# Casts of half batches 5 to 7 in another order and place, three row squares moved: a windowed attention with an MLP behind it

## The chip, the cores and the metric

The kernel runs on one core of one Trainium2 chip. Its engines are PE (matmul), DVE (VectorE), ACT (ScalarE), POOL (GpSimd) and SP (SyncE); POOL and SP also issue DMAs, each in the order of its own instructions. The metric is the device time of one launch in microseconds, the median of several runs. The kernel before took 351.6 us (three runs: 351.6, 352.7, 348.52).

## What is computed

Inputs are q, k and v of 8 batches, 8 heads, 576 rows and head size 64 in float32, eight global row numbers, and the weights of an MLP (512 to 2048 to 512). Cut to what matters, the reference is:

```
scores = q @ k.T / 8
mask   = (|i - j| <= 32) or i is global or j is global
attn   = softmax(where(mask, scores, -1e9))
x      = attn @ v, the heads of a row side by side     # 4608 x 512
h      = x @ w_in                                      # 4608 x 2048
out    = (h * cos(h)) @ w_out                          # 4608 x 512, float32
```

## The kernel before

A *half* is four of a batch's eight heads; half s is half of batch s // 2, so there are 16. A *pair* is two heads; half s holds pairs 2s and 2s + 1, 32 in all. The MLP works on nine tiles of 512 rows. A *first-layer unit* (`one`) is four matmuls of 128x512 for one of the 16 slices of h of a tile (L764), the cosine on ACT (L770) and the product g on DVE (L771). A *second-layer unit* (`two`) is four matmuls of 128x512 into an output block (L802); each fourth ends the block, which DVE or ACT evicts and SP writes out.

Pairs 0 to 9 take a path of their own and run mostly at the front. For halves 5 to 15 the work of a half is, in order:

- **casts** (`cast_half(s, which)`): for each letter of `which` one DMA on POOL, which reads v, k or q of the half in float32 and writes it in fp16 to device memory. v is L268, k and q are L272.
- **bring** (`bring(s)`), all on SP: a transposing DMA of k into kT (L284) and of q into qT (L285), which wait for k's and q's casts, and then the loads of v's windows for the two pairs (`load_v`, L350 to L357) and of its global rows (`load_vg`, L416), which wait for v's cast. kT and qT have two buffers each.
- per pair `local_k` (L609) and `local_q` (L621): DVE copies the windows out of kT and qT into kw and qb; POOL puts the global rows in their place (L581, L588).
- `scores` (L701 on PE, exponential on ACT at L704 and L709, mask multiply on DVE at L705 and L710, result pm), `values` (L721 on PE, normalised by DVE into xn at L732), `turn_x` (PE transposes xn at L746, DVE evicts it into xT at L748 and L749; behind each fourth pair POOL adds eight copies of global columns into xT, L754).
- `x_squares(s)` (L820): ACT squares the half's xn in place and adds the squares up, for a check at the end. xn has four buffers, one for each half.

The order of all this is written out by hand, as strings of steps that a loop at L1007 reads; each engine gets its instructions in this order and runs them in order, and semaphores join the engines. Step s = 4 reads MID (L50), 5 reads FIFTH (L52), 6 reads SIXTH (L54) and 7 to 15 read ORDER (L48). In them `1` is a first-layer unit and `2` a second-layer unit; `s`, `p`, `x`, `k`, `q` with a letter are scores, values, turn_x, local_k and local_q of pair 2s (`a`), 2s + 1 (`z`), 2s + 2 (`c`) or 2s + 3 (`d`); `n` is `x_squares(s - 1)` and `n1` is `x_squares(1)`; `G` (`casts(s)`) places the global rows of half s + 1 and, from step 6, a gate and the casts of half s + 2 in the order v, k, q; `Z0` to `Z5` build the masks of the second path on DVE; `A0` to `A2` gather the second half of the global rows on POOL; `K6` casts half 6; `B5` brings half 5, and `bring(s + 2)` is also called at the end of each step from 4 on (L1035).

`V10` and `U10` are gates. `hold(10)` (L391) and `hold_x(10)` (L395) are a copy of one element on POOL that waits until local_q, or the values, of pair 10 are done; POOL then goes on to the casts behind it. K5 stands at the end of FRONT, behind the 2 MB load of w_out; K6 stands in MID behind V10; K7 stands in FIFTH behind U10.

The `K` step is an entry of the table at L995, with the order of its three casts:

```
"K": lambda s: cast_half(s, "vkq")
```

Of the kernel before, what the change touches and what calls it, by code (L numbers as in the profile page):

```python
# [17 lines left out]
B, H, S, D = 8, 8, 576, 64  # L18
# [5 lines left out]
G = 8  # L24
# [17 lines left out]
C = G + QB  # L42
# [4 lines left out]

ORDER = "2 kz qz sa 2 2 2 sz pa 1 2 1 2 xa n pz 1 1 G 2 xz 1 1 2 kc qc 1 1"  # L48

MID = ("+ 1 1 1 1 Z0 1 1 1 Z1 1 1 Z2 1 1 A0 n1 1 Z3 1 1 1 Z4 1 1 A1 n2 1 1 1 Z5 A2 1 1 1 n3 B5 1 2 2 g10 g11 kc qc V10 K6 2 2 1 1 2 2 kd qd - 2 2")  # L50

FIFTH = "sa G 2 2 2 2 sz pa 1 1 2 xa U10 K7 pz 2 2 2 kc qc xz n kd qd"  # L52

SIXTH = "sa 2 2 2 2 sz pa 1 1 2 xa pz G 1 1 2 xz n 1 1 D0 2 kc qc D1 1 D2 2 1"  # L54

# [7 lines left out]
def view(ap, *dims):  # L63

    return bass.AP(ap.tensor, ap.offset, [ap.ap[0], *[list(d) for d in dims]])


def dview(ap, offset, *dims):

    return bass.AP(ap.tensor, ap.offset + offset, [list(d) for d in dims])  # L70
# [134 lines left out]
def kernel(  # L205
# [57 lines left out]
    def cast_half(s, which):  # L263

        base = s * 4 * S * D
        for x in which:
            if x == "v":
                nc.gpsimd.dma_start(v16[s * 4 * S : (s + 1) * 4 * S].rearrange("(n r) d -> n (r d)", r=16),  # L268
                                    dview(v, base, (16 * D, 4 * S // 16), (1, 16 * D)))
            else:  # L270
                src, dst = {"k": (k, k16), "q": (q, q16)}[x]
                nc.gpsimd.dma_start(dst[s].rearrange("t (h d) -> t h d", h=4),  # L272
                                    dview(src, base, (D, S), (S * D, 4), (1, D)))
# [41 lines left out]
    def warm(n, tag="s"):  # L315

        t = ps.tile([P, 4, P], FP32, tag=tag, bufs=2 + (tag == "s"))
        for _ in range(n):
            nc.tensor.matmul(t, ones16, view(ones16, (0, 4), (1, P)), start=True, stop=True)
# [436 lines left out]
    def mlp_in(t, f):  # L756
        if f == 0:
            g_of[t] = work.tile([P, NF, TT], FP16, tag="g", name="g")
        g16 = g_of[t]
        tag = "s" if spare[0] and f % 4 > 1 else "h"  # L760
        ph = ps.tile([P, TT], FP32, tag=tag, bufs={"s": 3, "h": 2}[tag], name="ph")
        ph_of.append((ph, g16[:, f]))
        for j in range(NC):
            nc.tensor.matmul(ph, w_in16[:, j, f * P : (f + 1) * P], xT[:, j, t * TT : (t + 1) * TT],  # L764
                             start=(j == 0), stop=(j == NC - 1))

    def mlp_act():
        ph, g = ph_of.pop(0)
        cos = work.tile([P, TT], FP16, tag="cos", bufs=3)
        nc.scalar.activation(cos, ph, AF.Sin, bias=pio2)  # L770
        nc.vector.tensor_tensor(g, cos, ph, ALU.mult)  # L771
# [99 lines left out]
    def one(act=True):  # L871
        for _ in range(1):

            if ins_q and ins_q[0][0] < ready[0] and ins_q[0][0] < outs_q[0][0] + 2:
                t, f = ins_q.pop(0)
                mlp_in(t, f)
                if act:
                    mlp_act()
                ready[1] = t * NF + f + 1
# [22 lines left out]
    with tc.manual_schedule():  # L902
# [85 lines left out]
        def bring(s):  # L988
# [4 lines left out]

        LOCAL = {"k": local_k, "q": local_q}
        OTHER = LOCAL | {"g": globals_kq, "L": load_qk, "W": load_w_in, "v": load_values, "n": x_squares,  # L995
                 "C": cast_vn, "I": row_numbers, "E": early_rows, "w": lambda n: warm(n, "h" if n == 6 else "s"), "y": value_rows, "M": next_values, "S": spread_vg, "V": hold, "U": hold_x, "H": early_globals, "Z": steady_buffers, "f": fill, "r": load_vn, "A": later_rows, "D": later_globals, "O": load_w_out, "K": lambda s: cast_half(s, "vkq"), "B": bring, "m": lambda _: one(False), "t": lambda _: mlp_act()}
        ready[0] = 1
        for step in FRONT.split():
            if step in "+-":
# [2 lines left out]
            f = (STEPS | OTHER)[step[0]]  # L1002
            f(*[int(x) for x in (step[1:] or "0").split(".")])
        ready[0], front[0] = 2, False
        for s in range(4, B * NP // 2):
            outs_by[0] = 8 * (s - 3)
            for step in {4: MID, 5: FIFTH, 6: SIXTH}.get(s, ORDER).split():  # L1007
                if step == "1":
# [19 lines left out]
                else:  # L1028
                    f, pr = (STEPS | OTHER)[step[0]], 2 * s + "azcd".index(step[1])
# [56 lines left out]
```

## Time and profile before

| | |
|---|---|
| median of three runs | 351.6 us |
| the profiled execution | 348.71 us |
| its span, first to last instruction | 346.9 us |
| mean granted clock of PE in it | 0.982 |
| PE busy | 329.1 us, 95% |
| DVE, ACT, POOL busy | 251.1, 241.6, 106.6 us |
| chain that ended last, share of PE | 80% |

A line of a timeline has the start in us from the span's start, the duration in us, the engine, the line of the kernel, the operation, what it writes and reads (out<-in, with partitions x elements), how many were merged, and in brackets how long the engine sat idle before it and what ended that. A line of the waits has the engine and the line that waited, for what, and us in total, times, and the longest. A line of busy times by stretch has the stretch, its length, the busy time of PE, of its weight loads, of DVE, ACT and POOL (number of instructions in brackets), the granted clock, the DMA share and GB/s. SPq is the queue of DMAs that SP issues.

In the profiled execution step 4 begins near 58.7 us, step 5 near 88.6, step 6 near 102.2, step 7 near 117.6; from there each step takes 16.65 us, until the attention ends near 268 us and only second- and first-layer units are left.

### The profile page before, as it was taken

The page shows a single profiled execution, that of the slowest core. Times are in us where ns is not written, and L with a number is a line of the kernel's source. Part 1 is how long each engine was busy: PE and PEld are TensorE (multiplying, and loading weights), DVE is VectorE, ACT ScalarE, POOL GpSimd, SP SyncE. Part 2 cuts the span into 40 slices and gives each one's busy share as a digit, 9 for nine tenths or more (in the row PEclk, how much of TensorE's full clock was granted, in tenths as well). Part 3 has the DMA queues.
Part 4 walks back from the last instruction along what each step waited for, and adds up shares of the span by engine and source line. Part 5 has one row for each costly group of instructions (what it writes and reads, how often), then busy time and mean ns, then how long its engine had stood idle before and what let it go on. Part 6 is the DMA issues. An engine that isn't in the chain of part 4 may idle for free.

```text
span 346.9 us, 8353 instructions
## 1 busy us (share of the span) xinstructions
PE 329.1 (95%) x3153; PEld 171.6 (49%) x3153; DVE 251.1 (72%) x610; ACT 241.6 (70%) x415; POOL 106.6 (31%) x218
## 2 busy tenths in 40 slices
PE   7986979999989999999999999999999999999993
PEld 3565865444444454545454545454545444444442
DVE  6668697987587688878787878788888466556310
ACT  8787684895566896878787777878787866644300
POOL 7846458333252506050705162324001000000000
PEclk9999698999999999999999999999999999999998
DMA  5999996999999999999999999999960001000112
GB/s 79 187 177 160 154 195 85 210 157 117 177 136 198 149 172 128 177 141 196 141 188 142 190 135 200 157 148 161 166 124 4 30 32 60 30 33 30 60 62 69
DMA packets 166275, 44.74 MB, mean 129 GB/s; under 512 B 153828, under 2 KB 161380, under 8 KB 166052
## 3 DMA queue, kind: packets, MB, share of 16 engines
q1 hardware_dynamic: 106244, 26.86, 52.6%
q0 software_dynamic: 59984, 17.28, 51.2%
q8 instruction: 27, 0.44, 0.6%
q14 instruction: 20, 0.16, 0.2%
HBM read 44.41 MB, written 19.17 MB: 183 GB/s over the span
## 4 chain that ended last, share of the span: by engine, by line
PE 80%; DVE 5%; DMA 4%; issue 3%; SPq 3%; ACT 3%; POOL 0%; POOLq 0%; ACTq 0%; DVEq 0%
PE po L802 34%; PE ph L764 34%; PE pv L721 3%; PE st L701 3%; DMA qn<-in_q_dram 2%; SPq L373 2%; PE tx L746 2%; DMA vn<-vg 2%; PE pv L648 1%; DVE g L771 1%; PE po L784 1%; ACT cos L770 1%; PE tx L680 1%; PE bank L597 1%; DVE pm L637 0%
## 5 line engine op out<-in xcount | busy, mean ns | idle before, releaser
L764 PE MATMUL ph<-xT,w_in 128*128 128x512 f16 x576 | 140.4, 382 | 1.1 <-DVE g L771 1.0
L770 ACT ACTIVATE cos<-ph,pio 128x512 f16<-128x512 f32 x144 | 97.1, 687 | 58.1 <-PE ph L764 54.2
L802 PE MATMUL po<-w_out,g 128*128 128x512 f16 x560 | 136.8, 379 | 0.0
L771 DVE TENSOR_TENSOR g<-cos,ph 128x512 f16<-128x512 f16 x144 | 96.5, 685 | 45.8 <-ACT cos L770 43.6
L764 PEld LDWEIGHTS <-w_in 128*128 128x128 f16 x576 | 54.2, 98 | 63.5 <-issue 3.0
L802 PEld LDWEIGHTS <-g 128*128 128x128 f16 x560 | 53.7, 98 | 63.7
L704 ACT ACTIVATE e<-st 128x512 f16<-128x512 f32 x44 | 23.9, 594 | 10.0 <-PE st L701 9.9
L705 DVE TENSOR_TENSOR pm<-e,mask 128x512 f16<-128x512 f16 x44 | 18.8, 427 | 11.7 <-ACT e L704 10.3
L981 POOL COPY gate<-xn 1x1 f16<-1x1 f16 x8 | 1.4, 180 | 81.9 <-DVE xn L732 81.9
L754 POOL COPY xT<-xg 128x4 f16 x48 | 15.6, 325 | 31.7 <-DVE xT L749 29.0
L272 POOL DMA_DIRECT2D q<-in_q_dram x11 | 24.0, 2180 | 0.0
L820 ACT ACTIVATE xn<-xn 128x1536 f16<-128x1536 f16 (+1 forms) x16 | 22.7, 1416 | 0.0
L732 DVE TENSOR_TENSOR xn<-pv,r_all 128x768 f16<-128x768 f32 x22 | 21.1, 958 | 1.0
L807 ACT COPY o<-po 128x512 f32<-128x512 f32 x17 | 10.0, 586 | 14.7 <-PE po L802 14.7
L809 DVE COPY o<-po 128x512 f32<-128x512 f32 x18 | 12.4, 690 | 9.0 <-PE po L802 8.5
L272 POOL DMA_DIRECT2D k<-in_k_dram x11 | 18.1, 1643 | 0.9 <-issue 0.9
L770 ACT ACT_TABLE_LOAD x12 | 15.4, 1283 | 0.2
L636 ACT ACTIVATE e<-st 128x488 f16<-128x488 f32 x20 | 10.5, 578 | 6.4 <-PE st L633 6.4
L704 ACT ACT_TABLE_LOAD x11 | 14.1, 1283 | 0.2
L609 DVE COPY kw<-kT 128x1320 f16<-128x1320 f16 x22 | 14.2, 646 | 0.0
L701 PEld LDWEIGHTS <-kw 64*128 64x128 f16 x484 | 8.4, 95 | 10.7 <-issue 8.1
L581 POOL COPY kw<-kgT 128x88 f16<-128x88 f16 x22 | 12.6, 706 | 0.2 <-ACT kgT L559 0.2
(184 smaller groups left out, 381.2 us busy)
## 6 DMA issues: line engine op xcount, KB each, us to landing
out_dram<-o SPq DMA_DIRECT2D x35, 256.0 KB
vw<-v SPq DMA_DIRECT2D x32, 165.0 KB
v<-in_v_dram POOLq DMA_DIRECT2D x11, 288.0 KB
k<-in_k_dram POOLq DMA_DIRECT2D x11, 288.0 KB
q<-in_q_dram POOLq DMA_DIRECT2D x11, 288.0 KB
vn<-in_v_dram SPq DMA_DIRECT2D x20, 120.0 KB
w_in<-in_moe_w_in_dram POOLq DMA_DIRECT2D x4, 512.0 KB
w_out<-in_moe_w_out_dram POOLq DMA_DIRECT2D x1, 2048.0 KB
```

Source lines behind the costliest of these rows:

```text
L272: nc.gpsimd.dma_start(dst[s].rearrange("t (h d) -> t h d", h=4), dview(src, base, (D, S), (S * D, 4), (1, D)))
L609: nc.vector.tensor_copy(to, view(kT[pr // 2 % 2][:, pr % 2], (QB, NB), (1, W)))
L701: nc.tensor.matmul(st[j // 8 * 2 + h][:, j % 8 * C : j % 8 * C + C], kp[hp, j], qp[hp, j], start=True, stop=True)
L704: nc.scalar.activation(e[:, 0:512], st[h], AF.Exp, scale=scale)
L705: nc.vector.tensor_tensor(view(pm[:, h], (1, 512)), e[:, 0:512], view(mask, (1, 512)), ALU.mult)
L732: nc.vector.tensor_tensor(view(xn, (384, 2), (D, 6), (1, D)), view(pv, (512, 2), (65, 6), (1, D)), view(rp, (6, 2), (1, 6), (0, D)), ALU.mult)
L754: nc.gpsimd.tensor_copy(xT[:, :, bass.ds(pool_idx[g] + b * S, 1)], xg[:, :, g : g + 1])
L764: nc.tensor.matmul(ph, w_in16[:, j, f * P : (f + 1) * P], xT[:, j, t * TT : (t + 1) * TT], start=(j == 0), stop=(j == NC - 1))
L770: nc.scalar.activation(cos, ph, AF.Sin, bias=pio2)
L771: nc.vector.tensor_tensor(g, cos, ph, ALU.mult)
L802: nc.tensor.matmul(po, g16[:, f, s * P : (s + 1) * P], w_out16[:, f], start=(f == 0), stop=(f == NF - 1))
L820: nc.scalar.activation(view(xn, (BP * P, 2), (1, n)), view(xn, (BP * P, 2), (1, n)), AF.Square, accum_out=x_sq[:, s : s + 1])
```

## The change

Three strings change.

```diff
-MID = ("+ 1 1 1 1 Z0 1 1 1 Z1 1 1 Z2 1 1 A0 n1 1 Z3 1 1 1 Z4 1 1 A1 n2 1 1 1 Z5 A2 1 1 1 n3 B5 1 2 2 g10 g11 kc qc V10 K6 2 2 1 1 2 2 kd qd - 2 2")
+MID = '+ 1 1 1 1 Z0 1 1 1 Z1 1 1 Z2 1 1 A0 1 Z3 1 1 1 n1 Z4 1 1 A1 1 1 1 Z5 A2 1 1 1 B5 1 2 2 g10 g11 kc qc V10 K6 n2 2 2 1 1 2 2 n3 kd qd - 2 2'
-FIFTH = "sa G 2 2 2 2 sz pa 1 1 2 xa U10 K7 pz 2 2 2 kc qc xz n kd qd"
+FIFTH = 'sa G 2 2 2 2 sz pa 1 1 2 xa pz 2 2 2 kc qc xz U11 K7 n kd qd'
-"K": lambda s: cast_half(s, "vkq")
+"K": lambda s: cast_half(s, "kqv")
```

- In MID the squares of half 1 move four first-layer units later, behind Z3; those of half 2 move from ahead of six first-layer units to behind K6, ahead of two second-layer units; those of half 3 move from ahead of B5 to behind four second-layer units, ahead of local_k of pair 11.
- In FIFTH the gate and the casts of half 7 move from behind the turn of pair 10 to behind the turn of pair 11, with its eight copies on POOL, and the gate waits for the values of pair 11 in place of pair 10.
- The casts of halves 5, 6 and 7 go out in the order k, q, v. Those of halves 8 to 15 keep v, k, q.

No instruction is added or taken away.

More of the change, by code (lines that the diff above doesn't have):

```diff
@@ L995 @@
         OTHER = LOCAL | {"g": globals_kq, "L": load_qk, "W": load_w_in, "v": load_values, "n": x_squares,
-                 "C": cast_vn, "I": row_numbers, "E": early_rows, "w": lambda n: warm(n, "h" if n == 6 else "s"), "y": value_rows, "M": next_values, "S": spread_vg, "V": hold, "U": hold_x, "H": early_globals, "Z": steady_buffers, "f": fill, "r": load_vn, "A": later_rows, "D": later_globals, "O": load_w_out, "K": lambda s: cast_half(s, "vkq"), "B": bring, "m": lambda _: one(False), "t": lambda _: mlp_act()}
+                 "C": cast_vn, "I": row_numbers, "E": early_rows, "w": lambda n: warm(n, "h" if n == 6 else "s"), "y": value_rows, "M": next_values, "S": spread_vg, "V": hold, "U": hold_x, "H": early_globals, "Z": steady_buffers, "f": fill, "r": load_vn, "A": later_rows, "D": later_globals, "O": load_w_out, "K": lambda s: cast_half(s, "kqv"), "B": bring, "m": lambda _: one(False), "t": lambda _: mlp_act()}
         ready[0] = 1
```

## Prediction

> **What bounds the kernel now.** I read the page first, then the busy times by stretch of the span, then who PE waited for between 52 and 130 us (the stretch in which the changed steps run), then the timelines of the five engines there. The first two show that PE has next to no free time.
>
> ```profile
> span 346.9 us, 8353 instructions
> PE 329.1 (95%) x3153; PEld 171.6 (49%) x3153; DVE 251.1 (72%) x610; ACT 241.6 (70%) x415; POOL 106.6 (31%) x218
> 96.00:104.00 8.00, 6.87 (x79) 3.65 (x78) 7.09 (x15) 4.90 (x8) 5.10 (x9) 1.00 1.53 146
> 153.00:267.00 114.00, 114.00 (x1138) 57.85 (x1137) 94.80 (x214) 89.58 (x145) 31.20 (x68) 1.00 1.40 152
> ```
>
> From 153 to 267 us PE is busy in all of the 114.00 us at a granted clock of 1.00, so nothing done by another engine there sets the end. Between 96 and 104 us 1.13 us of PE are missing. All that PE waited for other engines between 52 and 130 us is this:
>
> ```profile
> PE st L701 <- DVE qb L621: 1.1, 1, 1.1
> PE st L701 <- ACT o L807: 0.3, 1, 0.3
> PE ph L764 <- DVE g L771: 0.3, 1, 0.3
> ```
>
> The sum is 1.7 us (columns: total, times, longest). This is the most that a new order of steps 4 to 6 can win, since PE's own work is not changed and later stages start when PE gets there. It is 0.5% of the time: no gain over 2% is to be had here, and 2% (7 us) is about what a measurement of this kernel can tell from no change. A loss has no such ceiling.
>
> **The change part by part.**
>
> *The copy that waits for POOL (the largest term).* At the end of step 5 PE's scores of pair 12 wait for VectorE, which copies kw and qb of that pair. Rows picked from the timelines, VectorE first, then PE, then POOL (start us, us), then the group of all such copies, then a second case in step 4:
>
> ```profile
> 100.30 1.36 DVE L609 COPY kw<-kT 128x1320 f16<-128x1320 f16 x1
> 101.59 0.45 DVE L621 COPY qb<-qT 128x616 f16<-128x616 f16 x1
> 102.08 0.46 DVE L749 COPY xT<-tx 128x616 f16<-128x616 f16 x1
> 102.18 0.67 PE L701 MATMUL st<-qb,kw 64*128 64x64 f16 x22 [1.13 <-DVE qb L621]
> 97.09 0.18 POOL L395 COPY gate<-xn 1x1 f16<-1x1 f16 x1 [7.98 <-DVE xn L732]
> 97.54 0.52 POOL L268 DMA_DIRECT2D v<-in_v_dram  x1 [0.27 <-issue]
> 99.12 2.19 POOL L272 DMA_DIRECT2D q<-in_q_dram  x1
> 102.60 2.43 POOL L754 COPY xT<-xg 128x4 f16 x8 [1.30 <-DVE xT L749]
> L609 DVE COPY kw<-kT x22: 518/526/1850, 82.4 to 254.8; 128x1320 f16<-128x1320 f16 x22
> its engine sat idle before it (us, times) until:
> 86.62 1.85 DVE L609 COPY kw<-kT 128x1320 f16<-128x1320 f16 x1
> 85.93 2.19 POOL L272 DMA_DIRECT2D q<-in_q_dram  x1
> ```
>
> The kw copy takes 526 ns by its median over 22, but 1.36 us at 100.30 and 1.85 us at 86.62. Both ran while POOL was issuing a cast of q: that issue ends at 99.12 + 2.19 = 101.31 and the copy at 101.66; the other ends at 88.12 and its copy at 88.47. The copy ends 0.35 us behind the issue both times, so it is held until POOL is done. The change takes half 7's casts (U10 K7) from before pair 11's values to behind pair 11's turn (U11 K7 after xz), so at 100.30 POOL issues nothing. The copy then costs its median: 1.365 - 0.526 = 0.84 us less. qb starts at 100.75 in place of 101.59, and PE's scores at 101.34 in place of 102.18. PE is free from 102.18 - 1.13 = 101.05, so 0.29 us of the wait stays, and 0.84 is won on the path. The ends for this term are 0 (the time is given back at the next wait, a rival below) and 1.13 (the whole wait).
>
> *What moving K7 costs.* Every instruction of it counts: a gate copy and three cast issues on POOL, and behind them, on SP, the two transposes and the value loads of half 7. POOL runs in order, and K7 now stands behind the eight xT copies of pair 11, which start when VectorE has evicted that pair's turn. That eviction comes 0.84 earlier (101.24 for 102.08), so the xT copies run from 101.76 to 104.19 (2.43 us), the gate opens at about 104.15, and the first cast is issued 0.45 later as before (97.54 - 97.09), at 104.6. Its wait is on pair 11's values and costs nothing by itself, since the xT copies ahead of it need that pair's turn anyhow. The first cast is 7.1 us later than in the kernel before. The pair globals of step 6, queued behind K7 on POOL, are wanted by scores at 121 us and have over 10 us. What must be in time is the transposed half: kT and qT of pair 14, copied by VectorE in step 6.
>
> ```profile
> SPq L285 <- DMA q<-in_q_dram: 0.8, 1, 0.8
> 110.52 1.28 SPq L285 DMA_TRANSPOSE qT<-q  x1
> 118.04 0.46 DVE L621 COPY qb<-qT 128x616 f16<-128x616 f16 x1
> 121.02 0.49 PE L701 MATMUL st<-qb,kw 64*128 64x64 f16 x22
> v<-in_v_dram POOLq DMA_DIRECT2D x11, 288.0 KB
> ```
>
> Before, q was the last of three casts and SP waited 0.8 us for it and then issued its transpose at 110.52. Now q is second. v's issue no longer stands ahead of it, so q is issued about 1.1 us behind the first cast, at 105.7 for 99.12: 6.6 later. If its landing moved by just that, the transpose would start at 117.1. But v's 288 KB no longer go ahead of it; at the 152 GB/s of the stretch from 153 to 267 us that is 1.9 us, an estimate, so I take 115.2. The bounds are 117.1 (v's going behind saves nothing) and about 113 (it saves twice that). From issue to landing of a transpose no row gives a time. It is at least its own 1.28 us and at most 118.04 - 110.52 = 7.5, since the use at 118.04 did not wait. I take 1.28 plus 288 KB at that rate, 3.2. Then qT is there at 118.4. VectorE would reach qb at 118.04 - 0.84 = 117.2, so it waits some 1.2 us there and ends qb at 118.9; PE wants qb for pair 14 at 121.02 - 0.84 = 120.2. So the lateness costs VectorE a wait and PE nothing: 0 us, with 1.3 us of cover left. This is the thin place of the change. The values of half 7 are cast last and loaded last, but values of pairs 14 and 15 run behind those scores, after 124 us; I cost them at nothing, and the same 5 us of lateness is covered there.
>
> *The order k, q, v for halves 5, 6 and 7.* The same three issues and bytes, in another order. SP takes k's and q's transposes ahead of the loads of v, so transposes may begin sooner. The quoted group of kw copies says what that is worth: in 22 copies VectorE never sat idle before one (the line of its idle times is empty), so no transposed half was ever late. For halves 5 and 6 it is worth 0; for half 7 it is the 1.9 us already counted.
>
> *Three squares of rows on ACT.* Their rows in the kernel before, with what surrounds them:
>
> ```profile
> 68.97 1.26 ACT L820 ACTIVATE xn<-xn 128x1280 f16<-128x1280 f16 x1
> 70.22 2.41 ACT L770 ACTIVATE cos<-ph,pio 128x512 f16<-128x512 f32 x4
> 71.53 0.79 DVE L456 TENSOR_TENSOR mask<-nk,band 128x616 f16<-128x616 f32 x1
> 72.24 1.88 DVE L771 TENSOR_TENSOR g<-cos,ph 128x512 f16<-128x512 f16 x3
> 72.98 7.10 PE L764 MATMUL ph<-xT,w_in 128*128 128x512 f16 x32 [0.32 <-DVE g L771]
> 74.62 1.26 ACT L820 ACTIVATE xn<-xn 128x1280 f16<-128x1280 f16 x1
> 84.43 0.69 ACT L770 ACTIVATE cos<-ph,pio 128x512 f16<-128x512 f32 x1 [2.67 <-PE ph L764]
> 88.75 0.59 ACT L807 COPY o<-po 128x512 f32<-128x512 f32 x1 [2.77 <-PE po L802]
> ```
>
> Each square holds ACT for 1.26 us (start to the next cos, 68.97 to 70.22). The first falls just ahead of the twelfth of the units and its cosines come late by that; VectorE then has a mask of 0.79 us at 71.53 as well, and its g ends so late that PE waits 0.32 us at 72.98. The change puts n1 three units behind that mask, so mask and square no longer meet: cos 12 starts 1.0 sooner, and the g that PE waits for is done by about 72, before PE wants it at 72.66. At its new place n1 meets mask part 4 alone, which VectorE does while it waits for ACT. I take the whole 0.32 as won. The ends are +0.32 (the same wait comes back behind unit 15) and -0.32. n2 and n3 go into holes: ACT is idle for 2.67 us before 84.43 and 2.77 before 88.75, and 1.26 fits in each, with the eviction at 88.75 not delayed; if these holes closed, each would cost up to 1.26. The third of PE's waits (0.3 on the eviction at L807) stays. The buffers that the squares free are wanted in steps 5 to 7, far behind, so nothing queues for them.
>
> *Sum.* The profiled execution took 348.71 us (span 346.9). 348.71 - 0.84 - 0.32 = 347.55. The runs shown are 351.6, 352.7 and 348.52, so that execution lies 2.9 below their median. The mean of the four is 350.4; with 1.16 off, I predict 349.2 for the median after.
>
> **The rivals.**
>
> *Half 7 comes late and PE waits (slower than before).* Place: qb of pair 14 in step 6. It decides once qT lands after 120.2 - 0.46 - 0.13 = 119.6, with 0.46 for qb and 0.13 from qb's end to the scores (101.59 + 0.45 to 102.18). With the late bound for q (117.1) and the longest landing (7.5) it lands at 124.6 and PE loses 5.0; half way, 2.5. In terms of the profiled execution that is 350.0, at most 352.5. For it: the first cast is 7.1 us later, and the margin of 7.5 us between transpose and use shrinks to 2. Against it: VectorE has 2.4 us more before PE needs qb, and v no longer goes ahead.
>
> *The gain is given back.* ACT's exponentials of pair 12 follow a table load that does not move, and PE's next scores need the banks that they free:
>
> ```profile
> 104.89 0.56 ACT L709 ACTIVATE e<-st 128x192 f16<-128x192 f32 x2
> 106.35 0.49 PE L701 MATMUL st<-qb,kw 64*128 64x64 f16 x22
> 104.55 0.94 DVE L705 TENSOR_TENSOR pm<-e,mask 128x512 f16<-128x512 f16 x2 [1.19 <-ACT e L704]
> ```
>
> The last exponential ends at 105.45; PE would get there at 106.35 - 0.84 = 105.51. The margin is 0.06 us, so part of the 0.84 can return; if all of it did, only the 0.32 is left, 348.4.
>
> *The mask multiply is held in the kw copy's place.* K7's issues now lie from 104.6 to about 108.4 (99.12 + 2.19 - 97.54 = 3.8 us), over the multiply of pair 12 at 104.55. If they held it as they held kw, pm would end near 108.4 + 0.4 in place of 105.84 and PE's values would wait some 2.8 us: 350.3. The rows of the front speak against it:
>
> ```profile
> 43.45 0.74 DVE L637 TENSOR_TENSOR pm<-e,qT 128x488 f16<-128x488 f16 x2
> 41.85 2.24 POOL L895 DMA_DIRECT2D w_in<-in_moe_w_in_dram  x3
> 39.33 1.56 DVE L637 TENSOR_TENSOR pm<-e,qT 128x488 f16<-128x488 f16 x2
> 39.04 1.25 POOL L404 CAST vw<-vn 128x1280 f16<-128x1280 f32 x1 [4.70 <-DMA vn<-vg]
> ```
>
> Two multiplies at 43.45 took 0.74 together, as ever, inside three issues of w_in (41.85 to 44.09); two at 39.33 took 1.56, held by a CAST on POOL until 40.29. [...]
>
> **How the numbers follow.** Forecast 0.60; gain given back 0.14; half 7 late 0.16; multiply held 0.03; something not seen 0.07. The range takes in the spread of the runs, which is wider than the terms: from 348.52 less all 1.7 of PE's waits, 346.8, rounded down to 346.5, to the highest run with nothing gained, 352.7. Faster by over 2% would need 7 us where 1.7 are to be had: 0.03, for a measurement that falls low. Slower by over 2% needs more than the late bound of half 7: 0.05. Within 2%: 0.92.
>
> **What would show it.** Right: kw of pair 12 near 0.53 us, PE's wait for qb of pair 12 near 0.3, no wait of PE for g near 73, K7's first cast near 104 with k in front, SP's transposes of half 7 near 112 to 115, and a PE without gaps from 120 on. Wrong: a wait of VectorE for a DMA at L609 or L621 in step 6 with a PE gap behind it, a multiply at L705 of over 1 us, or a new wait of PE for g in step 4.

## The result, and the profile after

The change is slower: 353.62 us median of 20 runs (350.44 to 357.0) against 351.71 for the kernel before (20 runs, 348.19 to 356.08). The ratio of these medians is 1.0054; the ratio that is given from here on compares only runs within 1.5% of the fastest of the same kernel, and it is 1.0069, with a 95% interval of 1.0045 to 1.0093. I had forecast 349.2 us, a small gain; the time is outside my range, though within 2% as most of my chance said. The profiled execution of the changed kernel has a span of 350.8 us against 346.9.

Page, busy time by stretch, and PE's waits between 58 and 150 us, of the changed kernel:

```profile
PE 327.5 (93%) x3153; PEld 170.7 (49%) x3153; DVE 248.8 (71%) x610; ACT 242.2 (69%) x415; POOL 105.4 (30%) x218
```

```profile
96.00:104.00 8.00, 7.70 (x82) 3.97 (x82) 6.93 (x19) 4.91 (x7) 1.19 (x5) 1.00 1.45 111
120.00:136.00 16.00, 12.39 (x141) 6.31 (x139) 10.74 (x26) 10.53 (x17) 0.18 (x1) 1.00 1.34 158
153.00:267.00 114.00, 114.00 (x1135) 57.71 (x1133) 94.43 (x213) 89.86 (x144) 34.70 (x70) 1.00 1.44 157
```

```profile
PE pv L721 <- DMA vw<-vg: 2.1, 2, 1.2
PE st L701 <- issue: 1.4, 1, 1.4
PE st L701 <- ACT o L807: 0.3, 1, 0.3
PE st L701 <- DVE qb L621: 0.3, 1, 0.3
```

Between 96 and 104 us PE now lacks 0.30 us where it lacked 1.13: the gain that I forecast is there. Between 120 and 136 us it lacks 3.61 us, where it lacked nothing. Two waits make it up: 1.4 us before scores, 2.1 us before values. The attention's later steps and the end are as long as before (114.00 of 114.00 us busy). A span also carries the scatter of the front: the first scores of step 5 begin at 88.64 us before, at 89.40 here, and between 84.85 and 91.07 in the profiles below. So I compare stretches that begin there.

| stretch, from the starts of the scores | before | changed |
|---|---|---|
| pair 10 to pair 12 (step 5) | 88.64 to 102.18: 13.54 | 89.40 to 102.10: 12.70 |
| pair 12 to pair 16 (steps 6 and 7) | 102.18 to 137.67: 35.49 | 102.10 to 141.55: 39.45 |

Step 5 gains 0.84 us, as forecast to the digit; steps 6 and 7 lose 3.96. Step 4 gains 0.50 (from its first units, 58.69 to 88.64 before and 59.95 to 89.40 now). The sum is a loss of 2.6 us, or 0.75%, and the timed runs say 0.69%. That the two agree so closely is partly luck: in a second profile of the kernel before (e11, below) steps 6 and 7 took 38.03 us, and against that one the same sum is a loss of 0.1 us.

Where it is lost, in the changed kernel: POOL, then SP, VectorE and PE.

```profile
104.91 1.60 POOL L272 DMA_DIRECT2D k<-in_k_dram  x1
114.08 0.51 POOL L268 DMA_DIRECT2D v<-in_v_dram  x1 [0.27 <-issue]
115.65 2.21 POOL L272 DMA_DIRECT2D q<-in_q_dram  x1
```

```profile
SPq L284 <- DMA k<-in_k_dram: 5.6, 1, 5.6
```

```profile
112.77 2.26 SPq L284 DMA_TRANSPOSE kT<-k  x1
115.12 1.35 SPq L285 DMA_TRANSPOSE qT<-q  x1
119.20 4.04 SPq L416 DMA_DIRECT2D vw<-vg  x2
```

```profile
101.05 0.52 DVE L609 COPY kw<-kT 128x1320 f16<-128x1320 f16 x1
119.22 0.53 DVE L609 COPY kw<-kT 128x1320 f16<-128x1320 f16 x1 [1.74 <-DMA kT<-k]
121.73 0.47 DVE L621 COPY qb<-qT 128x616 f16<-128x616 f16 x1 [1.98 <-DMA qT<-q]
```

```profile
122.31 0.79 PE L701 MATMUL st<-qb,kw 64*128 64x64 f16 x22 [1.42 <-issue]
127.46 0.22 PE L721 MATMUL pv<-vw,pm 128*64 128x65 f16 x2 [1.24 <-DMA vw<-vg]
128.50 0.51 PE L721 MATMUL pv<-vw,pm 128*64 128x65 f16 x20 [0.82 <-DMA vw<-vg]
```

Half 7's first cast is issued at 104.91. SP waits 5.6 us for k to land and transposes it at 112.77, q at 115.12. VectorE copies kw only at 119.22, after 1.74 us of waiting for kT, and qb at 121.73, after 1.98 more for qT; in the profiled execution of the kernel before VectorE never waited for a transposed half. The scores begin when qb ends. (The wait of 1.42 us is put down to "issue" there; qb's end at 122.20 is what the start at 122.31 follows.) Then the value loads of pair 14, which SP issues behind those transposes (the last two of them, of the global rows, at 119.20), land late too, and PE waits 1.24 and 0.82 us for them.

### The profile page after: what moved, and what is told of

It is laid out like the page before. It is cut to its first block, busy times and chain, and to the rows that moved or that the text cites. A ratio compares the mean times of both kernels' runs of the same rounds, so it can differ in the third digit from the quotient of the medians.

```text
span 350.8 us, 8354 instructions
## 1 busy us (share of the span) xinstructions
PE 327.5 (93%) x3153; PEld 170.7 (49%) x3153; DVE 248.8 (71%) x610; ACT 242.2 (69%) x415; POOL 105.4 (30%) x218
## 4 chain that ended last, share of the span: by engine, by line
PE 80%; DMA 6%; DVE 5%; ACT 4%; issue 2%; SPq 1%; POOL 1%; ACTq 0%; POOLq 0%
PE ph L764 35%; PE po L802 31%; PE pv L721 3%; DMA qn<-in_q_dram 2%; PE st L701 2%; PE tx L746 2%; DMA vw<-vg 2%; DMA kn<-in_k_dram 2%; PE pv L648 1%; PE t L319 1%; PE po L784 1%; SPq L416 1%; PE bank L597 1%; DVE xn L668 1%; DVE pm L641 1%
## 5 line engine op out<-in xcount | busy, mean ns | idle before, releaser
L721 PE MATMUL pv<-vw,pm 128*64 128x65 f16 x484 | 12.6, 197 | 2.1 <-DMA vw<-vg 2.1
L581 POOL COPY kw<-kgT 128x88 f16<-128x88 f16 x22 | 14.3, 861 | 0.0
```

Of the source, the lines that this page charges most:

```text
L721: nc.tensor.matmul(pv[r0 : r0 + C, j // 6, c0 : c0 + 65], pm[:, h, j], vp[:, j, h], start=True, stop=True)
```

## The experiments

All were measured against the kernel before. For each I give the ratio with its interval, and from its profile the two stretches of the table above. The kernel before has 13.54 and 35.5 us there, the change 12.70 and 39.5.

**Half 7's casts put back (e1), made later still (e5), and moved alone (e2).** Theory 1 is that the lateness of half 7 is the loss; theory 2 blames the order of the casts, theory 3 the moved squares.

```diff
 e1, against the change
-FIFTH = 'sa G 2 2 2 2 sz pa 1 1 2 xa pz 2 2 2 kc qc xz U11 K7 n kd qd'
+FIFTH = 'sa G 2 2 2 2 sz pa 1 1 2 xa U10 K7 pz 2 2 2 kc qc xz n kd qd'
 e5, against the change (Y12: gate on the masked scores of pair 12; B7 left out of the end of step 5)
-FIFTH = '... kc qc xz U11 K7 n kd qd'
+FIFTH = '... kc qc xz n kd qd'
-SIXTH = "sa 2 2 2 2 ..."
+SIXTH = "sa Y12 K7 B7 2 2 2 2 ..."
 e2, against the kernel before
-FIFTH = "sa G 2 2 2 2 sz pa 1 1 2 xa U10 K7 pz 2 2 2 kc qc xz n kd qd"
+FIFTH = 'sa G 2 2 2 2 sz pa 1 1 2 xa pz 2 2 2 kc qc xz U11 K7 n kd qd'
```

> The changed kernel with half 7's gate and casts put back to where they were (before pair 11's values); the new places of the squares and the order k, q, v are kept. Theory 1 (half 7's casts are late, its transposed copies land after VectorE wants them, and PE stands 3.6 us between 120 and 136 us): that idle time is gone, the kw copy of pair 12 is held again (about 1.3 us), PE's wait for g in step 4 stays away; 0.3 to 0.5 us faster than before, ratio 0.998 to 1.000. Theory 2 (the order of the casts: v last makes the value loads late): the ratio stays at 1.003 or more and PE still waits for vw. Theory 3 (the moved squares cost): the ratio stays near 1.007.

> The changed kernel with half 7's casts later still: in step 6, behind a gate on the masked scores of pair 12, some 2 us behind their place in the change; half 7 is brought right behind. Theory 1: each us of lateness is a us of PE, so PE stands 5 to 6 us between 120 and 138 us in place of 3.6, and the ratio is about 1.012. Theories 2 and 3: no more than the change, 1.007.

> The kernel before with only half 7's gate and casts moved behind pair 11's turn; order v, k, q and the squares as before. Theory 1: as slow as the change or slower, since k and q now go behind v: qT lands some 2 us later than in the change, PE stands 4 to 6 us between 118 and 136 us, ratio 1.008 to 1.014; the wait for vw gets smaller, since v is first. Theory 2 (the order does it): within 0.2% of before. Theory 3 (the squares): within 0.2% of before.

e2: 1.0125 (1.0059 to 1.0191), stretches 12.69 and 41.31. e5: 1.0122 (1.0055 to 1.0189), 12.70 and 43.27. e1: 1.0019 (0.9975 to 1.0063), 13.03 and 39.56. Waits of VectorE and PE in e2, then in e5 (whose line numbers, like those of the kernels with the gate Y11, are four higher from L397 on):

```profile
DVE qb L621 <- DMA qT<-q: 4.7, 1, 4.7
```

```profile
PE st L701 <- issue: 4.0, 1, 4.0
```

```profile
DVE qb L625 <- DMA qT<-q: 3.5, 1, 3.5
```

```profile
PE st L705 <- issue: 4.6, 1, 4.6
```

The lateness alone, without the other two edits, loses at least as much as the whole change (41.31 us against 39.45; the intervals of the two ratios overlap). In e2, counted from the scores of pair 12, q's transpose is issued only 0.5 us later than in the change (13.56 us against 13.02), but it lands 8.6 us after its issue in place of 6.6 (114.86 to 123.49), and VectorE waits 4.7 us for qT:

```profile
114.86 2.24 SPq L285 DMA_TRANSPOSE qT<-q  x1
123.49 0.47 DVE L621 COPY qb<-qT 128x616 f16<-128x616 f16 x1 [4.69 <-DMA qT<-q]
```

PE's wait grows from 1.4 to 4.6 us when the casts go later still. So the lateness is enough for the loss, and theories 2 and 3 are not needed for it; that the order or the squares add a little is not excluded (e7 and e3 below). In e1 no half is late in step 7, as theory 1 has it, but its profile is not faster in steps 6 and 7. Another wait has come in step 6, and something behind it:

```profile
111.46 0.75 PE L721 MATMUL pv<-vw,pm 128*64 128x65 f16 x22 [2.42 <-DMA vw<-vg]
112.14 3.53 PE L764 MATMUL ph<-xT,w_in 128*128 128x512 f16 x8
116.71 1.89 PE L764 MATMUL ph<-xT,w_in 128*128 128x512 f16 x8
```

```profile
112.00:120.00 8.00, 7.90 (x45) 3.35 (x39) 4.68 (x11) 4.68 (x9) 3.97 (x4) 0.79 1.33 165
```

PE waits 2.42 us for value loads of half 6 (pair 13), and the eight matmuls behind that take 3.53 us where the next eight take 1.89, at a granted clock of 0.79 over the stretch. With what steps 4 and 5 win, this execution would be some 3 us slower, or 0.9%; the interval of e1's ratio ends at 1.0063, so I take this for what some executions do and not all.

**Each edit alone, and an earlier gate (e3, e7, e4, e6, e8).** The gate Y11 copies one element of pm of pair 11 on POOL, so that half 7's casts start some 1.5 us sooner and POOL is done before pair 12's kw copy.

```diff
 e3: of the change's edits only MID         e7: of them only "vkq" -> "kqv"
 e4, against the change
-FIFTH = '... xa pz 2 2 2 kc qc xz U11 K7 n kd qd'
+FIFTH = '... xa Y11 K7 pz 2 2 2 kc qc xz n kd qd'
 e6, against e4: the casts in the order v, k, q;  e8: half 7 alone in the order k, q, v
+    def hold_pm(pr):
+        nc.gpsimd.tensor_copy(gate, pm_of[pr][0:1, 1, NB - 1, C - 1 : C])
```

> The kernel before with only the three squares moved; order v, k, q and half 7's casts as before. Theory 1 (the lateness of half 7 is the loss, the squares are a small gain): PE's wait for g in step 4 is gone, PE waits about 1.1 us for qb of pair 12 as before, nothing for vw; ratio 0.998 to 1.000. Theory 3 (the squares cost): over 1.003.

> The kernel before with only the order of the casts of halves 5 to 7 changed to k, q, v. New theory 4, from the two experiments with early casts: with k and q of half 7 first, their small packets run beside the last value loads of half 6, so PE waits some 2 us for vw of pair 13 in step 6 and its granted clock falls behind that; ratio 1.002 to 1.010. Rival (that wait was due to the moved squares or the moved casts): no wait for vw, ratio 0.998 to 1.002.

> The changed kernel with half 7's casts in their old place, behind a gate that waits for the masked scores of pair 11 in place of the values of pair 10 (about 1.5 us sooner). Theory 1, and the reading that an issue on POOL holds the kw copy: the issues end before pair 12's kw copy begins, so that copy takes about 0.53 us, PE waits 0.3 us for qb of pair 12, and nothing is late in step 7; 1.2 us faster than before, ratio 0.995 to 0.998. If the casts must not meet the loads of half 6 on the DMA engines (a rival), half 6's or 7's loads come late and the ratio is over 1.000.

> The squares moved as in the change, half 7's casts in their old place behind the earlier gate (masked scores of pair 11), order v, k, q as before. Theory 4: v first leaves half 6's value loads some 2 us, so PE does not wait for vw in step 6; the kw copy of pair 12 is free (0.53 us), PE waits 0.3 us for qb of pair 12, and 1.2 us are won; ratio 0.995 to 0.998. Rival (the early gate alone brings the collision): PE waits 2 us or more for vw in step 6, ratio 0.998 to 1.003.

> The same as the kernel with the earlier gate and order v, k, q, but half 7 alone in the order k, q, v. Theory 4: it is half 7's order that makes the collision, so the wait for vw in step 6 is there again (2 us or more, and the clock falls behind it); 0.2 to 0.5% slower than with v, k, q. Rival (it is half 6's own v, cast last, that is late): no wait for vw in step 6, ratio 0.995 to 0.998.

> The same kernel as e8_pm_k7_kqv, once more: its interval excluded 1.000 while its profile shows 1.0 us of PE waiting for vw, so that no more than 0.5 us should be won. If the profile is right, ratio 0.997 to 1.001; if it truly is a version that beats both, 0.992 to 0.996 again.

> The same kernel as e6_pm_vkq, once more beside it on the same chip: squares moved, earlier gate, order v, k, q. By its profile 1.1 us are won up to step 8: ratio 0.996 to 0.999. If what is won is given back in waits for vw in later steps: 0.999 to 1.002.

| | ratio (interval) | step 5 | steps 6 and 7 |
|---|---|---|---|
| e3 squares only | 1.0038 (0.9997 to 1.0080) | 13.54 | 35.80 |
| e7 order only | 1.0057 (1.0014 to 1.0101) | 13.03 | 36.35 |
| e4 change, earlier gate | 0.9985 (0.9944 to 1.0026) | 12.69 | 39.62 |
| e6 the same, v k q | 1.0005 (0.9967 to 1.0043) | 12.70 | 35.74 |
| e6b once more | 0.9962 (0.9927 to 0.9998) | 12.70 | 35.36 |
| e8 half 7 k q v | 0.9937 (0.9887 to 0.9987) | 12.70 | 36.51 |
| e8b once more | 1.0020 (0.9988 to 1.0053) | 13.15 | 39.76 |

The squares alone win in step 4 (0.5 us in e3's profile) and cost nothing behind it; e3's timed ratio does not show the gain: it lies over 1.003, where theory 3 had it, though its interval just reaches no change. With order k, q, v the kw copy of pair 12 is held less even at the old place, and step 5 gains 0.51 in e7: the copy ends at 102.29, 0.36 us behind the end of q's issue (101.93), while v's issue, now last, goes on to 102.44. But PE then waits in step 6, 0.8 us and not the 2 that theory 4 had:

```profile
PE pv L721 <- DMA vw<-vg: 0.8, 1, 0.8
```

e7's interval lies above 1.000, but its profile accounts for 0.1% only (0.51 us won in step 5, 0.86 lost in steps 6 and 7). With the squares (e1), and with the squares and the earlier gate (e4), the same order has intervals that include 1.000, so whether the order alone costs a little stays open.

e6b is the kernel that I was after, with PE waiting for nothing from step 4 to the end but these three (the first at 270 us, behind the attention):

```profile
PE ph L768 <- DVE g L775: 0.6, 1, 0.6
PE st L705 <- ACT o L811: 0.3, 1, 0.3
PE st L705 <- DVE qb L625: 0.3, 1, 0.3
```

Theory 4, that half 7's order alone makes the collision with half 6's loads, is not shown: the wait in step 6 was 2.5 us in e4, 0.3 in the first profile of e6, none in e6b, 1.0 in e8, and 3.1 in e8b, so the same kernel has it or not. That may also be why e8's ratio, 0.9937 where I expected it above e6's, did not come again.

**What makes the transposes slow (e9), and a smaller lateness (e10).**

```diff
 e9, against the change: half 8's casts later, order k q v up to half 7, v k q from 8
-SIXTH = "... D0 2 kc qc D1 1 D2 2 1"
+SIXTH = "... D0 2 kc qc V14 K8 D1 1 D2 2 1"
-            if 5 < s < 2 * B - 2:
+            if 6 < s < 2 * B - 2:
 e10, against the change
-FIFTH = '... 2 2 2 kc qc xz U11 K7 n kd qd'
+FIFTH = '... 2 2 2 kc qc V12 K7 xz n kd qd'
```

> The change, with half 8's casts moved from step 6's middle to behind local_q of pair 14 (about 4 us later), so that they are not on the queues while half 7's transposes run; order and place of half 7 as in the change. If a transpose takes 6.5 us from issue to landing because half 8's casts run beside it: it lands in about 4 us, VectorE's waits for kT and qT in step 6 (1.7 and 2.0 us) mostly go, PE stands less than 2 us in step 7 in place of 3.5; ratio 0.999 to 1.003. Rival (a transpose takes this long by itself, or beside half 7's own v): landing stays at 6 us or more, ratio 1.005 to 1.010. If half 8 is then late itself, PE waits in step 8.

> The change, with half 7's casts half as late: in step 5 behind local_q of pair 12 and ahead of the turn of pair 11, some 3.5 us sooner than in the change. Theory 1 (lateness costs PE once the cover is used up): VectorE's wait for qT in step 6 is under 0.5 us and PE's stand in step 7 under 1 us. Given back: the kw copy of pair 13 is held behind the issues (about 3 us in place of 0.5), and the xT copies start some 3 us later, at most 1 us of it seen by PE. Ratio 0.998 to 1.003. Rival (late is late: any place behind the kw copy of pair 12 costs the same): 1.006 or more.

e9: 1.0005 (0.9960 to 1.0050), 12.70 and 37.57. Its transposes and the copies that wait for them:

```profile
110.39 2.08 SPq L284 DMA_TRANSPOSE kT<-k  x1
112.56 1.61 SPq L285 DMA_TRANSPOSE qT<-q  x1
```

```profile
115.00 0.53 DVE L609 COPY kw<-kT 128x1320 f16<-128x1320 f16 x1 [0.23 <-DMA kT<-k]
116.25 0.47 DVE L621 COPY qb<-qT 128x616 f16<-128x616 f16 x1 [0.72 <-DMA qT<-q]
118.68 2.77 DVE L609 COPY kw<-kT 128x1320 f16<-128x1320 f16 x1
```

With half 8's casts off the queues, kT is there 4.6 us after its issue and qT 3.7 after, where the change takes 6.4 and 6.6 (112.77 to 119.22, 115.12 to 121.73); VectorE's waits fall from 1.74 and 1.98 to 0.23 and 0.72. Half 7's own casts and transposes stand where they stand in the change, so most of the long landing there is the company of half 8's casts. (e9 is one execution; with half 8's casts in their old place the landings that VectorE waited for took 5.5 to 8.9 us in e2, e5, e10, e10b and e12.) By which mechanism the casts slow a transpose no run here shows. What is won in steps 6 and 7 (1.9 us) is lost again: half 8's casts, issued from 117 on, hold pair 15's kw copy for 2.77 us, and half 8's loads are late in step 8, which takes 20.58 us (136.96 to 157.54) in place of 16.65:

```profile
142.54 0.78 PE L721 MATMUL pv<-vw,pm 128*64 128x65 f16 x22 [1.96 <-DMA vw<-vg]
```

So e9 shows what slows the transposes, and not a faster kernel: the median of its runs is 352.54 us, of the kernel before beside it 350.55.

e10: 0.9943 (0.9906 to 0.9980), 12.70 and 37.25. Its first cast of half 7 is issued 13.17 us behind the first scores of step 5, where the kernel before has 8.90 and the change 15.51, so it is two thirds as late as the change and not half. VectorE waits only 1.0 us for qT, scores of pair 14 not at all, and the kw copy of pair 13 began just ahead of the issues and was not held. What it costs most is one wait, larger than the 1 us that I expected:

```profile
DVE qb L621 <- DMA qT<-q: 1.0, 1, 1.0
```

```profile
PE ph L764 <- POOL xT L754: 1.7, 1, 1.7
```

**How far a ratio can be trusted (e11, e12, e10b).** The kernel before against itself, the change again and e10 again, on one chip.

> The kernel before, unchanged, measured against itself. It must come out at 1.000; how far it lies off is the scatter that a ratio of 12 runs has here. From the one pair of repeats so far (0.9937 and 1.0020) I expect up to 0.4% off either way, with stage lengths in its profile as in the first (35.5 us from step 6 to step 8).

> The change itself, beside the other two. Theory 1: PE stands 3 to 4 us in step 7 again and steps 6 and 7 take about 39 us in place of 35.5; ratio 1.003 to 1.010. Rival (its loss was a draw of the front's scatter): steps 6 and 7 near 36 us, ratio 0.997 to 1.002.

> The kernel with half 7's casts half as late, once more. If the profile is right (1.75 us of PE waiting for the xT copies, 1.3 us won before): ratio 0.999 to 1.004, steps 6 and 7 about 37 us. If the first timing is right: 0.992 to 0.996 again, and the wait for xT is gone in this profile.

e11: 0.9986 (0.9947 to 1.0025), 13.54 and 38.03. e12: 1.0078 (1.0037 to 1.0118), 12.70 and 39.73. e10b: 0.9980 (0.9948 to 1.0012), 12.70 and 38.98. The change is slower by the same amount again, and PE again waits 3.5 us for half 7 (2.00 and 1.46 in e12, 1.42 and 2.06 in the first profile), which it does in neither profile of the kernel before. The second profile of the kernel before is the surprise:

```profile
PE pv L721 <- DMA vw<-vg: 2.6, 2, 1.5
```

PE waited 2.6 us for value loads of half 6 in an execution of the kernel before. The execution that I predicted from had none: it was a lucky one in step 6. Over all profiles this wait was 0 to 3.1 us in the ten whose casts of half 7 go out ahead of the scores of pair 12, and 0 to 0.3 us in the seven where they go out behind them. So the later casts also took away a wait, which the prediction did not count; that the early casts themselves make half 6's loads late is a reading that no run here tests by itself.

e10 is at 0.9943 and 0.9980, e6 at 1.0005 and 0.9962. Both are faster than the change, e10 clearly. That e10 beats the kernel before is likely, by 0.2 to 0.6% if its two ratios are taken as they are, but it is not settled by these runs.

## Why the prediction was wrong, point by point

- *The kw copy held by POOL*: right, and to size. 0.52 us in place of 1.36, PE's wait 0.30 in place of 1.13, step 5 shorter by 0.84, in the change and in e2, e4, e5, e6, e9, e10.
- *The squares*: right in kind, 0.50 us won in step 4 where I took 0.32; what the other 0.18 is stays open.
- *Moving K7*: this is the step that failed. I had half 7's first cast at 104.6 and it was issued at 104.91, in a kernel that ran 0.76 us later than my clock (scores of pair 12 at 102.10 for 101.34), so 0.45 sooner than I had it. q's transpose, 115.2 with me, came at 115.12, so 0.8 sooner. What failed is the sentence "I take 1.28 plus 288 KB at that rate, 3.2". Landing took 6.4 and 6.6 us, near the far bound of 7.5. I reckoned a transpose as if it had the DMA engines to itself; from 114 to 118 us half 8's casts were issued beside it, and e9, with 4.6 and 3.7 us where they were not, shows that they are most of it. qT was there at 121.73, or 120.97 in my clock, past the point, 119.6, at which I had written that PE would stand; the difference, 1.4 us, is PE's wait before those scores.
- *The value loads behind it* ("I cost them at nothing"): 2.06 us of PE, the larger of the two waits. I named when the values run and no time at which the loads would land. SP issued the loads behind q's transpose, and they were late with it: the transpose went out at 115.12 where the kernel before has 110.52, the last two loads for pair 14 from 119.20 on where it has 113.41, and PE waited for them until 128.50.
- *The order k, q, v*: "worth 0" for halves 5 and 6 holds within the scatter; for half 7 I had counted 1.9 us in the start of q's transpose. Without the order (e2) that start is only 0.5 us later, but the transpose takes 2.0 us longer from issue to landing, so the wait for qT is 2.7 us longer: the size is near mine, by another way than mine. It also shortened the hold of kw at the old place (e7, 0.51), which I had not seen.
- *The multiply under K7's issues*: not held, as the front's rows said. This is the pair of multiplies in the changed kernel, while POOL issued from 104.91:

```profile
105.29 0.91 DVE L705 TENSOR_TENSOR pm<-e,mask 128x512 f16<-128x512 f16 x2 [2.02 <-ACT e L704]
```

- *The gain given back at the next scores*: it was not; the second scores of step 6 begin 4.16 us after the first (102.10 to 106.26), as before (102.18 to 106.35, 4.17).
- *The rival "half 7 comes late and PE waits"* is what happened: I gave it 0.16 and 350.0 in terms of the profiled execution, half-way between its bounds; with the 2.6 us that the stretches lost it is 351.3. Its price was right to 1.3 us, partly by luck: it counted 2.5 us for qT, which cost 1.4, and nothing for the value loads, which cost 2.1. Its chance was too low, since the two bounds lay on either side of the point that decided and I had no row for a landing in company.
- *The base*: one execution without a wait for vw in step 6. In another the kernel before has 2.6 us there, so the cover in step 6 that the trace showed was thinner than it looked. The start of the sum was low too: of the 4.4 us between 349.2 and 353.62, 1.3 are that the kernel before has a median of 351.71 over 20 runs, where I began from 350.4. And a loss of 0.7% could be told apart, where I had written that 2% is about what a measurement can tell.

## What to carry to other kernels

When a transfer is moved later, find what else will be on the DMA queues at its new time: the time from a transpose's issue to its landing, 3.7 to 4.6 us without the next half's casts beside it (e9), was 6.4 and 6.6 with them (the change). What SP issued behind the late transposes went out late as well (the last loads for pair 14 at 119.20 in place of 113.41), and PE waited 2.06 us for it, so price the last load of that queue too, not only the first consumer. And where a transfer has to dodge a short hold (0.84 us), look for the smallest move that does it: casts just behind the copy that was held (e10), or ahead of it (e6), lost less than casts behind the whole pair.

## What the runs showed of the hardware

- A copy of 128x1320 fp16 in SBUF on VectorE was held while POOL issued the casts of k and q (2.77 us in e9, 0.52 when free): it ended 0.35 or 0.36 us behind the end of q's issue, in the kernel before (101.66 behind 101.31, 88.47 behind 88.12), in e7 (102.29 behind 101.93) and in e9 (121.45 behind 121.09). v's issue behind q's did not hold it in e7 (it went on to 102.44), and a multiply of two SBUF tiles was not held (0.91 for two at 105.29 in the change, while POOL issued, and 0.91 for two at 107.42 in the kernel before, while it did not).
- PE's granted clock was lower behind some of the waits of about 2 to 4 us: 0.79 over the eight us behind 2.42 us of waiting in e1, and 0.57 over four behind 3.98 in e2; the 12 matmuls behind the latter took 4.30 us where the same 12 took 2.76 in the kernel before (at 121.44). Behind 2.00 us of waiting in e12 the same 12 took 2.76, but behind 1.96 us in e9 the clock was 0.90 over the 17 us from 136, and four matmuls at 144.33 took 1.91 us where four at 136.00 took 1.03, so the length of the wait alone did not decide it.

```profile
124.00:128.00 4.00, 3.81 (x30) 1.70 (x31) 2.91 (x7) 1.53 (x4) 0.00 (x0) 0.57 1.40 105
```

```profile
118.64 0.79 PE L701 MATMUL st<-qb,kw 64*128 64x64 f16 x22 [2.00 <-issue]
119.37 2.76 PE L802 MATMUL po<-w_out,g 128*128 128x512 f16 x12
```

- Two executions of one kernel differed in steps 6 and 7 by 2.5 us for the kernel before (35.5 and 38.0, with 0 and 2.6 us of PE's waiting for value loads) and by 3.3 for e8 (36.5 and 39.8, with 1.0 and 3.1 us, and eight matmuls behind the wait in 1.90 and 3.25), beside the scatter of the front. A single profile showed one of these and not the other.
